# Pooled attention with a routed MLP on one core: the second batch's stores on GpSimd, and another order of all engines' work

## The chip, the cores and the metric

The kernel runs on 1 core of one Trainium2 chip. The metric is device time in microseconds (us): 264.95 us, the median of 3 runs (262.59 to 265.17).

The core has five engines that work beside each other and meet through semaphores. PE (TensorE) multiplies matrices, and its weight loads are listed apart as PEld. DVE (VectorE) and ACT (ScalarE) do elementwise work. POOL (GpSimd) does small elementwise work and issues gathers, scatters and accumulating loads. SP (SyncE) issues plain DMAs. Each engine takes its own instructions strictly in the order of the program: an instruction that waits holds everything that stands behind it on that engine. DMA transfers themselves run on 16 DMA engines that all issuers share.

## What is computed

The input is q, k and v of 8 batches, 8 heads, 576 tokens and a head size of 64, all float32. Keys and values are averaged over groups of 8 tokens, so that 72 pooled ones are left. Each token attends to them. The heads are joined to rows of 512, a gate scores each row, and the 128 best rows of each batch go through a two-layer MLP (512 to 1024 to 512), scaled by a sigmoid of the score and added back.

```
k_p, v_p = mean of k, v over groups of 8 tokens          # 576 -> 72
attn     = softmax(q @ k_p.T / 8) @ v_p                   # per batch and head
x        = attn, heads joined                             # (8, 576, 512)
scores   = x @ w_gate;  top = 128 best tokens per batch
out      = x;  out[top] = x[top] + sigmoid(scores[top]) * (relu(x[top] @ w1) @ w2)
```

## The kernel before

The batches are numbered 0 to 7 here, so the "second batch" is batch 1. Each batch passes two halves.

The **front** of a batch b: its k, q and v are loaded by SP (the last part of v comes in two pieces, of which POOL issues the second, with an add, L346). DVE pools k (L364, L365) and transposes it (L370, L377, L380), transposes q in two halves (L385), and pools v (L423 to L435). PE makes the scores in four quarters (L399), ACT takes their exponentials (L408). A small product centres the gate column (L441). PE then forms the attention output in five chunks (L463; the fifth is a half chunk), ACT and DVE normalise each chunk (L479 to L487) into a result tile `xs`, and each chunk is stored to the output in HBM (L262: four stores of 256 KB and two of 64 KB per batch). From the gate scores (L508 to L515) PE spreads a row over all partitions (L535, two pieces: one of three transposes and one of two), ACT counts ranks (L547), DVE makes a one-hot matrix (L551), PE picks the tokens with it (L560), POOL turns them into row indices (L569) and gathers the 128 chosen rows from HBM (L570). The gather waits until all six stores of its batch have landed.

The **dense half**: PE transposes the gathered rows (L589), multiplies by w1 in eight steps ("up", L597), ACT applies relu (L602), PE multiplies by w2 in eight steps ("down", L606), DVE adds (L611), and POOL scatters the rows back (L615). The weights w1 and w2 are loaded in two halves each. w1's second half is used first.

All these steps are recorded first, as 754 numbered operations with their data dependences (`Plan`), and then emitted in the order that the table `ORDER` gives, so one table sets the order on every engine and on every queue. The table `BANKS` says which bank of PSUM each step takes. The planner knows no times: it places what the table says. 24 small products with zeros (`heat` L278, `fill` L284), which compute nothing, are placed by the table as well, among PE's first work.

Which engine issues a batch's stores is set in `attend`:

```
STORE = ("POOL", "ACT")
...
by = STORE[b] if b < len(STORE) else "SP"
```

So batch 0's stores are issued by POOL, batch 1's by ACT, and those of all others by SP. DMAs that are issued by SP and ACT take turns on one set of eight semaphores (named DMAHW0 to DMAHW7 in the built program), those by POOL on another set of eight (DMASW0 to DMASW7). A DMA whose turn falls on a semaphore is issued only after the DMA that had it before has landed, and its issuer waits for that.

After the scatter of the last batches a range test decides whether a general path has to run; with these inputs it does not.

Of the kernel before, what the change touches and what calls it, by code (L numbers as in the profile page):

```python
# [15 lines left out]
@with_exitstack  # L16
def kernel(
    ctx: ExitStack,
    tc: tile.TileContext,
    q: bass.AP,  # L20
    k: bass.AP,
    v: bass.AP,
    moe_w_gate: bass.AP,
    moe_w1: bass.AP,
    moe_w2: bass.AP,
    moe_capacity,
    out: bass.AP,
):

    nc = tc.nc
    args = (q, k, v, moe_w_gate, moe_w1, moe_w2, moe_capacity, out)
    flag = ctx.enter_context(tc.tile_pool(name="flag", bufs=1)).tile([1, 1], I32, name="flag")
    with ExitStack() as direct:
        direct_path(direct, tc, *args, flag)
    again = nc.values_load(flag[0:1, 0:1], min_val=0, max_val=1)  # L40
    with tc.If(again > 0):
        with ExitStack() as general:
            general_path(general, tc, *args)
# [55 lines left out]


ORDER = [int(x) for x in """
# [27 lines left out]
""".split()]  # L129


BANKS = [int(x) for x in """
# [3 lines left out]
""".split()]  # L136


def direct_path(ctx, tc, q, k, v, moe_w_gate, moe_w1, moe_w2, moe_capacity, out, flag):
# [14 lines left out]
    ROWS = [128] * 4 + [64]  # L154
    HALF = ((0, 16), (16, TG))
    FILL = 16
    STORE = ("POOL", "ACT")
    POOLED = ("DVE",)
    VCUT = ((0, 4), (4, H))
    KCUT = ((0, 12), (12, 24), (24, TG))  # L160
# [287 lines left out]
    def attend(b, c):  # L448
# [46 lines left out]
        rows = out[b].rearrange("(g t) d -> g t d", g=G)  # L495
        by = STORE[b] if b < len(STORE) else "SP"
        if c < 4:
# [544 lines left out]
```

## Time and profile before

| what | before |
|---|---|
| median of 3 runs | 264.95 us (262.59 to 265.17) |
| the profiled execution | 264.21 us, its span 262.3 us |
| PE busy | 234.5 us, 89% of the span |
| DVE, ACT, POOL busy | 133.1, 104.7, 41.2 us |
| moved by DMA | 46.92 MB, 179 GB/s over the span |
| mean granted TensorE clock | 0.962 of full |

The span runs from the first instruction to the last, and 1.9 us lie around it in that execution. In the views a line such as L399 is a line of the kernel, a name such as `xs<-pA,rz` says what an instruction writes and reads, and `x32` that 32 records are taken together (one matrix product with float32 operands leaves two records). "SPq" or "ACTq" is an engine's sequencer, here issuing a DMA. In brackets stands the engine's idle time before the instruction, and who ended it. A granted clock of 1 is 2.4 GHz, 0.5 is 1.2 GHz.

### The profile page before, as it was taken

How to read it: one execution, taken by the hardware profiler on the slowest of the kernel's cores; microseconds unless marked ns; L12 is line 12 of the kernel's file. 1: busy time of each engine (PE TensorE's matmuls, PEld its weight loads, DVE VectorE, ACT ScalarE, POOL GpSimd, SP SyncE). 2: the span in 40 equal slices, each digit the busy share in tenths (PEclk: the TensorE clock that was granted, in tenths of full speed). 3: DMA queues.
4: the chain of work that ended last, by engine and by line, in shares of the span. 5: the costliest groups of instructions: out<-in, count | busy, mean ns of one | idle time of the engine just before them, and what ended most of it. 6: DMA issues, size and time to landing. Idle time of an engine off the chain costs nothing.

```text
span 262.3 us, 7033 instructions
## 1 busy us (share of the span) xinstructions
PE 234.5 (89%) x2994; PEld 179.2 (68%) x2994; DVE 133.1 (51%) x295; ACT 104.7 (40%) x262; POOL 41.2 (16%) x95
## 2 busy tenths in 40 slices
PE   7869969875982999999999998999999999999960
PEld 3348757764982866985689656967796695897420
DVE  4779599967512378569992294753402421100020
ACT  2033426834532466261368316437544453122000
POOL 3001313041001040003110126101101033300020
PEclk9997999999797799999999999999999999999995
DMA  7999999999999069909889974301001751200011
GB/s 216 261 340 285 244 301 347 238 366 340 378 233 339 4 123 329 220 6 317 272 273 281 245 265 100 122 2 42 4 0 42 227 176 40 80 4 1 4 44 42
DMA packets 22454, 46.92 MB, mean 179 GB/s; under 512 B 1904, under 2 KB 12016, under 8 KB 21520
## 3 DMA queue, kind: packets, MB, share of 16 engines
q1 hardware_dynamic: 18864, 38.80, 50.4%
q0 software_dynamic: 2816, 6.42, 9.3%
q10 hardware_dynamic: 736, 1.18, 1.4%
q8 instruction: 25, 0.41, 0.7%
q14 instruction: 13, 0.11, 0.1%
HBM read 34.87 MB, written 11.53 MB: 177 GB/s over the span
## 4 chain that ended last, share of the span: by engine, by line
PE 34%; issue 8%; DMA 4%; POOL 2%; DVE 1%; SPq 1%; POOLq 0%; DVEq 0%
PE pJ L597 13%; PE pJ L606 12%; PE pA L463 3%; PE pS L399 2%; DMA out_dram<-y,ix 2%; DMA vr<-in_v_dram 2%; PE pJ L535 1%; POOL vr L346 1%; PE pJ L589 1%; POOL out_dram L615 1%; SPq L262 1%; DVE y L611 1%; PE pJ L463 0%; POOL xr L570 0%; PE pJ L560 0%
## 5 line engine op out<-in xcount | busy, mean ns | idle before, releaser
L597 PE MATMUL pJ<-xg,w 128*128 128x128 f32 x512 | 63.6, 281 | 0.0
L597 PEld LDWEIGHTS pJ<-xg,w 128*128 128x128 f32 x512 | 60.4, 195 | 3.2 <-issue 1.9
L606 PE MATMUL pJ<-w,ht 128*128 128x512 f32 x128 | 60.1, 604 | 0.0
L408 ACT ACTIVATE et<-pS 128x1024 f32<-128x1024 f32 (+1 forms) x40 | 37.3, 937 | 39.5 <-PE pS L399 39.0
L399 PE MATMUL pS<-qt,kt 32*128 32x128 f32 (+1 forms) x1024 | 42.9, 304 | 3.8 <-issue 2.0
L399 PEld LDWEIGHTS pS<-qt,kt 32*128 32x128 f32 x1024 | 35.6, 192 | 10.0 <-issue 4.4
L463 PEld LDWEIGHTS pA<-vp,et 128*64 128x64 f32 x960 | 32.5, 144 | 6.4 <-issue 2.3
L606 PEld LDWEIGHTS pJ<-w,ht 128*128 128x128 f32 x128 | 22.5, 190 | 20.9 <-issue 20.1
L463 PE MATMUL pA<-vp,et 128*64 128x66 f32 x960 | 36.6, 232 | 0.2 <-issue 0.2
L547 ACT ACTIVATE cmp<-sr,sc 128x576 bf16<-128x576 f32 (+1 forms) x40 | 31.0, 776 | 3.8 <-issue 3.1
L487 DVE TENSOR_TENSOR xs<-pA,rz 128x512 f32<-128x512 f32 x30 | 20.7, 692 | 4.5 <-DVE rz L485 2.0
L385 DVE STREAM_TRANSPOSE qt<-qr 128x1024 f32<-128x1024 f32 (+1 forms) x16 | 21.9, 1368 | 1.0 <-DMA qr<-in_q_dram 1.0
L611 DVE SCALAR_TENSOR_TENSOR y<-pJ,gv,xr 128x512 f32<-128x512 f32 x8 | 6.0, 749 | 29.5 <-PE pJ L606 26.0
L485 DVE RECIPROCAL rz<-za 128x8 f32<-128x8 f32 (+1 forms) x40 | 7.7, 192 | 26.0 <-ACT za L479 25.8
L602 ACT ACTIVATE ht<-pJ 128x512 f32<-128x512 f32 x16 | 9.6, 598 | 26.1 <-PE pJ L597 26.1
L479 ACT ACTIVATE za<-pA,eps 128x8 f32<-128x8 f32 x30 | 8.0, 266 | 22.9 <-PE pA L463 22.6
L615 POOL DMA_INDIRECT out_dram<-y,ix x8 | 8.4, 1047 | 48.4 <-DVE gv L579 24.9
L569 POOL TENSOR_SCALAR ix<-tg 128x1 int32<-128x1 f32 x8 | 1.9, 237 | 83.4 <-DVE tg L565 82.3
L535 PE MATMUL pJ<-ident,sc 128*128 128x128 f32 (+1 forms) x40 | 8.3, 289 | 5.5 <-DVE sc L515 5.4
L540 ACT COPY sr<-pJ 128x192 f32<-128x192 f32 (+1 forms) x16 | 6.4, 398 | 15.5 <-PE pJ L535 15.5
L364 DVE TENSOR_TENSOR kr<-kr 128x1152 f32<-128x1152 f32 (+1 forms) x10 | 11.1, 1111 | 2.5 <-DMA kr<-in_k_dram 2.5
L346 POOL DMA_DIRECT2D vr<-in_v_dram x8 | 7.7, 1008 | 28.8 <-DMA vr<-in_v_dram 28.8
(84 smaller groups left out, 198.5 us busy)
## 6 DMA issues: line engine op xcount, KB each, us to landing
kr<-in_k_dram SPq DMA_DIRECT2D x7, 1152.0 KB, 11.4
vr<-in_v_dram SPq DMA_DIRECT2D x8, 896.0 KB, 15.1
out_dram<-xs SPq DMA_DIRECT2D x24, 256.0 KB, 5.2
qr<-in_q_dram SPq DMA_DIRECT2D x8, 640.0 KB, 11.8
qr<-in_q_dram SPq DMA_DIRECT2D x8, 512.0 KB, 11.3
w<-in_moe_w_dram SPq DMA_DIRECT2D x4, 1024.0 KB, 16.4
kr<-in_k_dram SPq DMA_DIRECT2D x3, 384.0 KB, 4.0
vr<-in_v_dram SPq DMA_DIRECT2D x8, 128.0 KB, 8.3
```

The costliest lines, as they stand in the source:

```text
L346: nc.gpsimd.dma_start(out=x[TWO:128], in_=rows_v(b, TWO + 1, 128 - TWO, 2), accum_op=OP.add)
L364: e.tensor_tensor(out=x[:, a:z, 0:2], in0=x[:, a:z, 0:2], in1=x[:, a:z, 2:4], op=OP.add)
L385: nc.vector.transpose(out=QT[b % 2][h].rearrange("p j s (t g) -> p t (j s) g", g=G), in_=QR[b % 2][h].rearrange("p t (j s g) -> p t (j s) ...
L399: nc.tensor.matmul(pS[:, i, 256 * s : 256 * s + n], KT[b % 2][p, j, s, :], QT[b % 2][h][p, j, s, x : x + n], start=(j == 0), stop=(j == 1))
L408: nc.scalar.activation(ET[c][b % NB[c]].rearrange("p n (g t) -> p n g t", g=G), pS.rearrange("p i (s x) -> p (i s) x", s=2)[:, :, y : y + ...
L463: nc.tensor.matmul(o[d][64 * w : 64 * w + 64, E * y : E * y + E], et[:, 2 * m + s, 64 * u : 64 * u + 64], VP[i][:, 2 * m + s, :], start=Tr ...
L487: nc.vector.tensor_tensor(out=XS[i][c].rearrange("p (m s d) -> p s m d", s=2, d=D)[:, k], in0=o[:, :, :, 0:D], in1=rz.rearrange("p (s m on ...
L535: nc.tensor.transpose(row[:, OFF[c] - OFF[a] : OFF[c] - OFF[a] + n], SC[i][0:n, c : c + 1].to_broadcast([n, 128]), ident[0:n, 0:n])
L547: nc.scalar.activation(cmp[0:n], SR[0:n], AF.Sign, bias=SC[i][0:n, c : c + 1], scale=-1.0, accum_out=RK[0:n, b, c])
L597: nc.tensor.matmul(acc[:, cap * f : cap * f + cap], w1[g][:, d, 128 * f : 128 * f + 128], XG[i][:, d, :], start=(d == 0), stop=(d == DB - 1))
L606: nc.tensor.matmul(job(ds)[0:cap, :], HT[i][f // 4][:, f % 4, :], w2[f // 4][:, f % 4, :], start=(f == 0), stop=(f == FB - 1))
L615: j = nc.gpsimd.indirect_dma_start(out=out_rows, out_offset=bass.IndirectOffsetOnAxis(ap=IX[x][:, :1], axis=0), in_=Y[i], in_offset=None)
```

## The change

The stores of batch 1 are issued by POOL instead of ACT, and the two tables are replaced as a whole. No operation is added or taken away, and none changes its size. The diff, with a line or two of each table:

```diff
 ORDER = [int(x) for x in """
-33 27 28 2 30 0 35 36 37 42 38 43 31 39 40 44 41 1 108 47 45 46 32 34 111 62 5 3 15 8 4 63 58 59 110 109 9 14
+2 28 33 27 4 19 14 9 35 36 37 16 18 12 17 30 7 31 42 43 44 0 32 34 38 39 6 21 25 24 40 41 45 46 47 1 108 48
...
 BANKS = [int(x) for x in """
-3 3 3 3 3 3 3 3 1 2 1 1 1 2 1 2 1 1 1 1 2 2 2 2 3 3 3 3 1 0 1 0 0 1 2 1 2 3 3 3 3 2 0 1 0 0 1 2 1 1 1 2 1 1 3
+3 3 3 3 3 3 3 3 2 1 1 1 2 1 1 1 1 1 1 1 1 1 1 1 3 3 3 3 1 0 0 0 1 1 1 2 2 3 3 3 3 1 0 0 0 0 1 2 1 2 2 1 2 2 3
...
-    STORE = ("POOL", "ACT")
+    STORE = ("POOL", "POOL")
```

On POOL the six stores of batch 1 now stand behind that batch's own small work (L520 to L524) and ahead of the accumulating load of batch 4 and of batch 1's gather.

The first place is ACT around batch 1's last stores. The rows name in brackets the semaphores that an instruction waits for. `xs_98` to `xs_102` are batch 1's five result chunks, `ss_103` the gate scores of batch 2, `et` the exponentials of batch 3, `cmp` the rank counts of batch 1. Before:

```order
L602 ACTIVATE ht_132<-pJ_163 128x512 [waits PE_49]
L262 DMA out_dram<-xs_100 16x8x512 [waits DMAHW0_49]
L408 ACTIVATE et_83<-pS 128x1024 [waits PE_49]
L262 DMA out_dram<-xs_98 16x8x512 [waits DMAHW4_49]
L262 DMA out_dram<-xs_99 16x8x512 [waits DMAHW6_49]
L547 ACTIVATE cmp,rk<-sr,sc_108 128x576 [waits Activation_49]
L262 DMA out_dram<-xs_102 16x4x256 [waits DMAHW0_49]
L511 COPY ss_103<-ss_103 64x4 [waits DVE_49]
L262 DMA out_dram<-xs_101 16x8x512 [waits DMAHW1_49]
L408 ACTIVATE et_85<-pS 128x1024 [waits PE_49]
```

With the change:

```order
L547 ACTIVATE cmp,rk<-sr,sc_108 128x576 [waits Activation_49]
L547 ACTIVATE cmp,rk<-sr,sc_108 64x576 [waits Activation_49]
L602 ACTIVATE ht_132<-pJ_164 128x512 [waits PE_49]
L408 ACTIVATE et_87<-pS 128x1024 [waits PE_49]
L479 ACTIVATE za<-pA,eps 128x8 [waits DVE_49,PE_49]
L480 COPY ss_103<-pA 128x8
L511 COPY ss_103<-ss_103 64x4
L479 ACTIVATE za<-pA,eps 128x8 [waits DVE_49,PE_49]
L480 COPY ss_103<-pA 128x8
```

What moved: the stores are gone from ACT, and the copy of `ss_103` (L511), which DVE needs for batch 2's row scores, no longer stands behind a DMA that waits for a DMAHW semaphore.

The second place is PE between batch 0's pick (L560, `oh`) and the transposes of its gathered rows (L589, `xr_125`). `vp_91` and `vp_90` are the pooled values of batch 1 and batch 2, `qt_78` and `qt_79` the two halves of batch 2's q, `pJ_163` and `pJ_164` two PSUM banks. Before:

```order
L560 MATMUL pJ_164<-aux_110,oh 128x9
L284 MATMUL pJ_163<-zero 128x256
L463 MATMUL pJ_163<-vp_91,et_85 64x66 x8
L463 MATMUL pJ_164<-vp_91,et_85 64x66 x8
L463 MATMUL pA<-vp_90,et_84 64x66 x16
L399 MATMUL pS<-qt_79,kt_76 128x192 x16
L463 MATMUL pA<-vp_90,et_86 64x66 x16
L535 MATMUL pJ_163<-ident,sc_108 128x128
L535 MATMUL pJ_163<-ident,sc_108 128x64
L589 MATMUL pJ_163<-ident,xr_125 128x128 x4
```

With the change, where one quarter of scores and one chunk of attention (`qt_78`, `et_88`) stand between the pick and the first row here:

```order
L284 MATMUL pJ_163<-zero 128x256
L399 MATMUL pS<-qt_79,kt_76 128x128 x16
L441 MATMUL pJ_163<-vp_90,share 128x8
L463 MATMUL pA<-vp_91,et_87 64x66 x16
L399 MATMUL pS<-qt_79,kt_76 128x192 x16
L535 MATMUL pJ_163<-ident,sc_108 128x128
L535 MATMUL pJ_163<-ident,sc_108 128x64
L535 MATMUL pJ_164<-ident,sc_108 128x128 x3
L463 MATMUL pA<-vp_90,et_82 64x66 x16
L463 MATMUL pJ_163<-vp_90,et_89 64x66 x8
L589 MATMUL pJ_164<-ident,xr_125 128x128 x4
```

What moved: the pick now stands ahead of six steps of batches 1 and 2 that it stood behind, and behind one chunk (`et_85`) that it stood ahead of. Between it and the transposes stand three quarters of scores and three full chunks of attention, where there were one quarter and three chunks.

The third place is SP where the weights are loaded: `w_138` and `w_137` are the second and the first half of w1, `w_139` and `w_140` those of w2, `kr`, `qr`, `vr` parts of k, q and v of batches 3 and 4. Before:

```order
L262 DMA w_138<-in_moe_w_dram 128x4x512
L262 DMA qr_70<-in_q_dram 128x1024
L262 DMA w_137<-in_moe_w_dram 128x4x512
L262 DMA qr_71<-in_q_dram 128x1280
L262 DMA w_139<-in_moe_w_dram 128x4x512
L262 DMA kr<-in_k_dram 128x2304
L262 DMA w_140<-in_moe_w_dram 128x4x512
L262 DMA qr_68<-in_q_dram 128x1024
L262 DMA vr_72<-in_v_dram 16x8x256
L262 DMA vr_72<-in_v_dram 112x8x256
```

With the change:

```order
L262 DMA w_138<-in_moe_w_dram 128x4x512
L262 DMA qr_71<-in_q_dram 128x1280
L262 DMA vr_73<-in_v_dram 112x8x256
L262 DMA w_137<-in_moe_w_dram 128x4x512
L262 DMA kr<-in_k_dram 128x2304
L262 DMA vr_72<-in_v_dram 16x8x256
L262 DMA w_139<-in_moe_w_dram 128x4x512
L262 DMA qr_68<-in_q_dram 128x1024
L262 DMA vr_72<-in_v_dram 112x8x256
L262 DMA w_140<-in_moe_w_dram 128x4x512
```

What moved: each weight half now stands behind more of the loads of batches 3 and 4, the last half of w2 behind batch 4's whole v.

## Rows read from the trace of the kernel before

**Rows 1.** 10 us stretches: engines busy (instructions); granted clock, DMA share, GB/s.
```profile
20.00:30.00 10.00, 9.76 (x198) 8.24 (x200) 8.53 (x16) 3.67 (x11) 0.96 (x2) 0.83 1.17 233
30.00:40.00 10.00, 7.96 (x158) 6.48 (x158) 7.70 (x14) 3.87 (x9) 3.78 (x7) 1.00 1.07 319
60.00:70.00 10.00, 6.98 (x86) 6.32 (x83) 6.05 (x12) 5.43 (x18) 1.01 (x5) 0.83 1.05 358
80.00:90.00 10.00, 6.65 (x88) 6.09 (x92) 3.44 (x6) 4.32 (x11) 1.01 (x5) 0.66 0.50 177
90.00:100.00 10.00, 10.00 (x127) 6.25 (x120) 6.97 (x14) 6.38 (x19) 3.23 (x4) 1.00 0.62 142
```

**Rows 2.** PE's timeline at 34 us: start, length, instruction [idle before, releaser].
```profile
34.96 0.94 PE L399 MATMUL pS<-qt,kt 32*128 32x128 f32 x21 [1.98 <-issue]
```

**Rows 3.** Timeline of all engines, 71 to 86 us; ACTq issues DMAs.
```profile
71.72 0.56 ACTq L262 DMA_DIRECT2D out_dram<-xs  x1
...
82.29 0.55 ACTq L262 DMA_DIRECT2D out_dram<-xs  x1
82.87 0.19 ACT L511 COPY ss<-ss 64x4 f32<-64x4 f32 x1 [5.00 <-DMA out_dram<-xs]
...
83.10 0.20 DVE L515 TENSOR_REDUCE sc<-ss 128x5 f32<-128x40 f32 x1 [6.88 <-ACT ss L511]
...
83.35 0.90 PE L535 MATMUL pJ<-ident,sc 128*128 128x128 f32 x3 [5.39 <-DVE sc L515]
...
84.05 1.91 PE L597 MATMUL pJ<-xg,w 128*128 128x128 f32 x8
...
85.89 2.09 PE L399 MATMUL pS<-qt,kt 32*128 32x128 f32 x32
```

**Rows 4.** DMA issues in four short stretches: KB each, us from issue to landing.
```profile
out_dram<-xs ACTq DMA_DIRECT2D x1, 256.0 KB, 10.5
...
xr<-out_dram,ix POOLq DMA_INDIRECT x1, 8.9
...
w<-in_moe_w_dram SPq DMA_DIRECT2D x1, 1024.0 KB, 17.5
...
vr<-in_v_dram SPq DMA_DIRECT2D x1, 896.0 KB, 18.7
```

**Rows 5.** SP's timeline: the issues of the last two transfers of Rows 4.
```profile
49.66 1.16 SPq L262 DMA_DIRECT2D w<-in_moe_w_dram  x1
...
61.19 1.36 SPq L262 DMA_DIRECT2D vr<-in_v_dram  x2
```

**Rows 6.** PE's timeline: the first centring, batch 0's pick and its gathered rows.
```profile
19.53 0.36 PE L441 MATMUL pJ<-vp,share 128*128 128x8 f32 x2 [2.52 <-DVE vp L435]
...
52.99 0.37 PE L560 MATMUL pJ<-aux,oh 128*128 128x9 bf16 x5
...
63.81 0.63 PE L589 MATMUL pJ<-ident,xr 128*128 128x128 f32 x4 [2.88 <-DMA xr<-out_dram,ix]
```

**Rows 7.** Timeline, 161 to 163 us.
```profile
161.51 0.75 DVE L611 SCALAR_TENSOR_TENSOR y<-pJ,gv,xr 128x512 f32<-128x512 f32 x1 [3.44 <-DMA out_dram<-y,ix]
...
162.32 0.39 PE L441 MATMUL pJ<-vp,share 128*128 128x8 f32 x2 [1.23 <-DVE gv L578]
```

**Rows 8.** Chain of waits, 182 to 206 us: PE's steps at full clock.
```profile
182.26 1.10 PE pS L399 x32
...
187.32 1.51 PE pS L399 x32
...
189.91 1.09 PE pJ L597 x8
...
200.19 1.08 PE pA L463 x32
...
205.65 1.05 PE pJ L606 x2
```

**Rows 9.** Line 262: POOL's stores, shortest/median/longest ns, first and last start.
```profile
L262 POOL DMA_DIRECT2D out_dram<-xs x6: 525/544/567, 29.9 to 39.6; - x6
```

56 rows, old and new, of tables (BANKS, ORDER) are left out of this document.

## The prediction

> **What bounds the kernel now.** I read the stretches first, then PE's timeline for its waits, then that of all engines around the longest of them. In the stretches [rows 1] PE is busy for all of 90 to 100 us, while the DMA engines are at 0.62: from there on the loads are ahead, and PE's own work sets the pace until the end. Before that the reader is to see two things: PE is busy for only 6.65 us of 80 to 90 and 6.98 of 60 to 70, and in the same stretches its granted clock is 0.66 and 0.83 of full. So the price of a wait is the wait itself and the half-speed work behind it.
>
> The longest wait is 5.39 us, at 83.35 [rows 3]. PE's spread of batch 2's row scores waits for DVE's sum, that for ACT's copy of the gate scores (L511), and that stood on ACT behind a store of batch 1. This store was issued at 82.29. The store issued at 71.72 had the same DMAHW semaphore and took 10.5 us to land [rows 3, 4], until 82.2. So ACT did nothing for 5.00 us because a DMA semaphore came round. The two next longest waits are 2.88 us for batch 0's gathered rows and 2.52 us for the first centring [rows 6].
>
> The sum is made against the profiled execution, 264.21 us with a span of 262.3. It is 0.74 below the median of the runs. I leave that inside the range.
>
> **The change part by part.** All of PE's, DVE's and ACT's operations stay as many and as large. After 90 us PE has one wait left, of 1.2 us [rows 7], so what is saved before it moves the end by as much.
>
> *Batch 1's stores off ACT.* The wait of 5.39 goes. With it goes the half-speed work: the spread took 0.90 for three transposes, the up step 1.91 and the scores 2.09 [rows 3], where an up step takes 1.09 and a quarter of scores 1.10 at full clock [rows 8]. That is 0.82 and 0.99, and half of 0.90 on the spread: 2.3. What is late next? The sum's other inputs are products that DVE makes itself; in the new order the first spread piece of batch 2 stands behind batch 1's pick and two more up steps, so I cost the remainder at 0. Together **-7.7**. Bounds: 0 if another wait takes the place, -7.7 at most.
>
> *The same six stores on POOL.* POOL issues a store in 0.525 to 0.567 us [rows 9], six in 3.3. POOL is busy for 1.01 us of 60 to 70 and of 80 to 90 [rows 1], so this lies beside other work. What is queued behind them on POOL are the accumulating load of batch 4, batch 1's gather and batch 2's small work. The gather must land before batch 1's transposes on PE. Between batch 1's pick and those the new order has two up steps, three chunks, two quarters and eight down steps among others, 2 x 1.09 + 3 x 1.08 + 2 x 1.10 + 8 x 1.05 = 16.0 us by [rows 8]. From batch 0's pick to its transposes it took 63.81 - 52.99 = 10.8 us [rows 6], with the DMA engines full. So 5.2 us of cover are left: **0**.
>
> The six stores that POOL issued before [rows 9] fell mostly into 30 to 40 us, where DVE was busy for 7.70 of 10 us [rows 1], and they lie within 8% of each other. The Trainium skill, "SBUF — State Buffer", section "SBUF: two separate sides", speaks against this change: DMAs issued from GpSimd need it to write their descriptors, it is locked out while VectorE runs certain operations, and such a DMA of about 620 ns then takes about 3100. By that page six stores would hold POOL for an estimated 18.6 us instead of 3.3, and the sum would be up to 10.1 us higher, by what exceeds the cover. The trace does not agree so far: no store of POOL shows it.
>
> *Batch 0's gathered rows.* The chain from pick to transposes took 10.8 us, most of it the gather's 8.9 us to land [rows 4, 6]. In the new order three quarters of scores (1.10, 1.10, 1.51), three chunks (1.08 each) [rows 8] and six small steps lie between. The small ones I estimate at 2.1 us, from the pick's 0.37 [rows 6] and the 0.90 at half clock for three transposes [rows 3]. That is 9.05, so 1.8 of wait remain and 1.1 go. With them goes the slow clock behind the wait: 0.83 over 10 us is 1.7 us [rows 1], of which I take 1.5, since PE was not busy throughout. I take it whole, because PE also waited 1.98 us at 34.96 [rows 2], and 30 to 40 us kept the full clock [rows 1], while 2.52, 2.88 and 5.39 were each followed by a slow one. **-2.6**. Bounds: 0, if the gather lands that much later with more stores on the way, and -4.4.
>
> *The first centring.* The new order puts the third quarter of scores of batch 0 ahead of it, 1.10 us of work that stood behind [rows 8]. The wait of 2.52 falls to 1.4, and by the same reasoning the slow clock of 20 to 30 us (0.83) [rows 1] goes: 1.5. **-2.6**. Bounds: 0, if the q transpose that this quarter needs comes late on DVE and PE only waits one step earlier, and -4.0.
>
> *The wait on a scatter.* At 162.32 PE waits 1.23 us behind DVE, which had waited 3.44 for batch 0's scatter to land before it could write its buffer again [rows 7]. On POOL that scatter stood behind batch 3's gather, batch 1's scatter and an accumulating load. Now it directly follows the gather, and between batch 3's pick and the end of batch 2's down steps PE has eight score and attention steps, where it had two. **-1.2**. Bounds: 0 to -1.2.
>
> *The weights, a new wait.* Every half of w1 and w2 stands later on SP. Before, w2's first half was issued at 49.66 and took 17.5 us, to 67.2; batch 4's v was issued by 62.5 at the latest and took 18.7, to at most 81.2 [rows 4, 5]. In the new order w1's first half has the same loads but one weight half ahead of it as the former had, w2's last half as much as the latter. Batch 1's stores, 1.15 MB, now go out before them: at 358 GB/s [rows 1] 3.2 us more. So they land by 70.4 and 84.4. When does PE ask? Batch 0's pick comes ahead of two quarters and three chunks and behind one: 2 x 1.10 + 2 x 1.08 = 4.4 us earlier, at 48.6, the transposes 10.8 later, at 59.4. The fifth up step follows three quarters, three chunks and four up steps, some 11 us: 70. The fifth down step follows four more up steps, three quarters, four chunks and four down steps, some 17: 87. A small wait is likely at the first, none at the second. The bounds are 0 and 3.5; I take **+1.0**, nearer to the lower end, since PE comes to each half at about its landing or later.
>
> The opening's zero products, the pause inside a step [rows 2] and the last four steps with the scatters behind them stay: 0 each, the pause of 2.0 both ways as a bound.
>
> The sum: 264.2 - 7.7 - 2.6 - 2.6 - 1.2 + 1.0 = **251.1**.
>
> **The rivals.** *The loads become the bound.* At 20 to 40 and 60 to 70 us the DMA engines are over 1.0 [rows 1], and the new order asks for batch 3's front and the weights in the same stretch. Two waits of 2.5 us at weights or scores, each with 1.5 of slow clock, give 251.1 + 8 = 259. For it: the DMA share. Against: at 80 to 90 it is 0.50 already. Chance 0.18, times 255 to 262.
>
> *POOL's issues go slow.* If POOL could write an issue only while DVE idles, six stores of 3.3 us would take 8.3 us where DVE is busy for 6.05 of 10 us, and 22 where it is busy for 8.53 [rows 1]: 5 to 19 us more, less the cover of 5.2, so 251 to 265, some 258 in the middle. Against: [rows 9], which were taken under a busy DVE. Chance 0.04. The rule of the Trainium skill, "SBUF — State Buffer", section "SBUF: two separate sides", is of this kind.
>
> *The change doesn't save what it says*: the loads, not ACT, set when 83 us is reached, and everything only waits elsewhere: 264. For it: batch 4's v lands close to that time, at 81. Against: the one long wait of that stretch was for ACT [rows 3]. Chance 0.06.
>
> *Slower: weights behind buffers on SP.* The last half of w2 now stands behind batch 4's q and v, which wait until batch 2's are no longer read. If DVE frees those late, SP holds the weights too, and PE stands at the fifth down step of batch 0 with nothing else allowed past. It decides from the point at which that half lands 16.5 us after PE's arrival, at 103.5 instead of 84.4: then 251.1 + 16.5 = 267.6. For it: such transfers took 17.5 and 18.7 us to land [rows 4], so that a late issue is paid in full. Against: DVE has to pool batch 2's v before any chunk of batch 2, which PE does before the first up step. With the half-speed work behind such a wait, 270. Chance 0.06.
>
> **The numbers.** My forecast has 0.66, and its own range is 246 to 255: below, the gathered rows' last 1.8, the +1.0 and the pause of 2.0 fall away; above, one of the two 2.6 terms stays and so does 1.3 more of weights. The range for 8 in 10 takes in both 2.6 terms lost and weights at 3.5, 251.1 + 2.6 + 2.6 + 2.5 = 258.8, which also covers over half of the first rival: 246 to 259. A measurement of this kernel can tell about 1% from no change, 2.6 us: 262.3 to 267.6. Faster: 0.66, 0.17 of the first rival and 0.03 of the second, 0.86. Same: the third, with the rest of the first two, 0.08. Slower: 0.06.
>
> **What would show it.** In the profile of the changed kernel ACT issues no DMA, and no copy of gate scores waits for one; the spread of batch 2 waits under 1 us. The stores on POOL take about 0.55 us each. The wait before batch 0's transposes is under 2 us, that before the first centring under 1.5, and 60 to 70 us and 80 to 90 us have a granted clock of 1.0. PE is busy throughout some 10 us sooner than at 90. Wrong it is if PE waits over 2 us for a weight half, if batch 1's gather is issued long after its pick, or if PE, though it is through batch 3's front early, waits for batch 5's loads.

## The result: 250.83 us, and where the 13.6 us came from

The changed kernel takes **250.83 us** (median of 4 runs, 249.48 to 255.33) against 264.42 beside it, a ratio of 0.948, with a 95% interval of 0.940 to 0.955. Measured again (e9) it took 251.54 (6 runs), 0.952 (0.948 to 0.957). The forecast was 251.1, with a range of 246 to 259. Some executions of most kernels here are over 1.5% above the fastest of the same kernel; the ratios leave them out, and the profiles of e1, e8 and e12 below are of such ones.

The profiled execution took 249.48 us, with a span of 247.7 and a mean granted clock of 0.991. The stretches come first, with the columns of [rows 1]:

```profile
20.00:30.00 10.00, 9.21 (x202) 7.02 (x198) 9.16 (x17) 4.01 (x13) 1.73 (x3) 1.00 1.08 286
30.00:40.00 10.00, 7.57 (x150) 5.97 (x146) 7.98 (x14) 4.95 (x11) 4.79 (x12) 1.00 1.06 300
...
60.00:70.00 10.00, 10.00 (x204) 9.21 (x197) 7.76 (x16) 7.67 (x21) 0.00 (x0) 1.00 1.03 398
...
80.00:90.00 10.00, 10.00 (x145) 6.42 (x144) 6.05 (x12) 3.17 (x7) 0.95 (x1) 1.00 0.86 272
90.00:100.00 10.00, 10.00 (x113) 9.20 (x113) 4.09 (x9) 5.70 (x15) 0.00 (x0) 1.00 1.04 282
```

The granted clock was 0.83, 0.83 and 0.66 at 20, 60 and 80 us [rows 1] and is 1.00 now. PE is full from 60 us on, while it was busy for 6.98 and 6.65 us of the stretches at 60 and 80. PE's timeline, at the places of [rows 3, 6]:

```profile
16.98 1.17 PE L399 MATMUL pS<-qt,kt 32*128 32x128 f32 x32 [1.63 <-DVE qt L385]
...
18.99 0.36 PE L441 MATMUL pJ<-vp,share 128*128 128x8 f32 x2 [0.21 <-DVE vp L435]
...
45.65 0.37 PE L560 MATMUL pJ<-aux,oh 128*128 128x9 bf16 x5 [0.45 <-DVE oh L551]
...
58.44 0.63 PE L589 MATMUL pJ<-ident,xr 128*128 128x128 f32 x4 [1.41 <-DMA xr<-out_dram,ix]
...
69.52 2.05 PE L597 MATMUL pJ<-xg,w 128*128 128x128 f32 x16
...
76.41 0.47 PE L535 MATMUL pJ<-ident,sc 128*128 128x128 f32 x2
...
86.61 0.54 PE L535 MATMUL pJ<-ident,sc 128*128 128x128 f32 x3
86.99 2.74 PE L606 MATMUL pJ<-w,ht 128*128 128x512 f32 x6
```

Both pieces of batch 2's spread (L535) start without a wait, where 5.39 us stood. The wait for batch 0's gathered rows is 1.41 us (2.88), that before the first centring 0.21 (2.52), but 1.63 now stands before the quarter that was put ahead of it. Neither half of the weights is waited for, at 69.52 (L597) and 86.99 (L606). The wait of 1.23 at 162 us [rows 7] is gone.

POOL, DVE and SP in the stretch of batch 1's stores:

```profile
56.15 3.17 POOL L262 DMA_DIRECT2D out_dram<-xs  x6
```
```profile
56.21 1.24 DVE L385 STREAM_TRANSPOSE qt<-qr 128x1024 f32<-128x1024 f32 x1
```
```profile
61.99 7.03 SPq L262 DMA_DIRECT2D w<-in_moe_w_dram  x1
```

Six stores in 3.17 us are 0.53 each, as in [rows 9], with DVE at work beside them. SP's issue of w2's last half, against that, took 7.03 us.

The span fell by 14.6 us. PE's busy time fell by 7.1, from 234.5 to 227.4, with the same products. In the three slow stretches of before PE was busy for 12.2 us at a granted clock of 0.50, which is 6.1 us lost, and the zero products went from 20.3 to 18.7 us. PE's idle time fell from 27.8 to 20.3: the four waits of [rows 3, 6, 7] went from 12.0 to 3.25, and the rest, of which the end behind PE's last product is 0.8, grew by 1.3.

### The profile page after: what moved, and what is told of

It is laid out like the page before. It is cut to its first block, busy times and chain, and to the rows that moved or that the text cites. A ratio compares the mean times of both kernels' runs of the same rounds, so it can differ in the third digit from the quotient of the medians.

```text
span 247.7 us, 7047 instructions
## 1 busy us (share of the span) xinstructions
PE 227.4 (92%) x2994; PEld 173.9 (70%) x2994; DVE 132.6 (54%) x294; ACT 104.2 (42%) x260; POOL 45.3 (18%) x101
## 4 chain that ended last, share of the span: by engine, by line
PE 71%; DMA 16%; issue 5%; DVE 3%; POOL 2%; SPq 1%; POOLq 0%; DVEq 0%
PE pJ L597 24%; PE pJ L606 22%; PE pA L463 10%; PE pS L399 10%; DMA vr<-in_v_dram 9%; DMA xr<-out_dram,ix 4%; DMA kr<-in_k_dram 2%; PE pJ L535 2%; PE pJ L589 2%; DMA out_dram<-y,ix 1%; PE pJ L463 1%; PE pJ L560 1%; POOL out_dram L262 1%; SPq L262 1%; DVE xs L487 1%
## 5 line engine op out<-in xcount | busy, mean ns | idle before, releaser
L597 PE MATMUL pJ<-xg,w 128*128 128x128 f32 x512 | 62.0, 278 | 0.0
L597 PEld LDWEIGHTS pJ<-xg,w 128*128 128x128 f32 x512 | 59.2, 192 | 3.1 <-issue 2.2
L606 PE MATMUL pJ<-w,ht 128*128 128x512 f32 x128 | 59.8, 602 | 0.0
L399 PE MATMUL pS<-qt,kt 32*128 32x128 f32 (+1 forms) x1024 | 41.3, 296 | 3.5 <-DVE qt L385 2.4
L399 PEld LDWEIGHTS pS<-qt,kt 32*128 32x128 f32 x1024 | 34.3, 185 | 10.6 <-issue 4.0
L463 PE MATMUL pA<-vp,et 128*64 128x66 f32 x992 | 36.0, 225 | 1.6 <-DVE xs L487 0.9
L606 PEld LDWEIGHTS pJ<-w,ht 128*128 128x128 f32 x128 | 22.5, 190 | 20.4 <-issue 19.8
L463 PEld LDWEIGHTS pA<-vp,et 128*64 128x64 f32 x992 | 31.7, 137 | 7.1 <-issue 3.1
L487 DVE TENSOR_TENSOR xs<-pA,rz 128x512 f32<-128x512 f32 x31 | 21.5, 692 | 5.0 <-DVE rz L485 2.0
L479 ACT ACTIVATE za<-pA,eps 128x8 f32<-128x8 f32 x31 | 8.3, 267 | 23.9 <-PE pA L463 23.2
L551 DVE TENSOR_TENSOR oh<-slots,rk 128x640 bf16<-128x640 f32 x8 | 6.6, 823 | 13.7 <-ACT cmp L547 13.7
L423 DVE TENSOR_TENSOR vr<-vr 128x1024 f32<-128x1024 f32 (+1 forms) x9 | 9.8, 1099 | 4.4 <-DMA vr<-in_v_dram 4.4
## 6 DMA issues: line engine op xcount, KB each, us to landing
qr<-in_q_dram SPq DMA_DIRECT2D x8, 640.0 KB, 10.8
w<-in_moe_w_dram SPq DMA_DIRECT2D x4, 1024.0 KB, 24.6
```

Source lines behind the costliest of these rows:

```text
L399: nc.tensor.matmul(pS[:, i, 256 * s : 256 * s + n], KT[b % 2][p, j, s, :], QT[b % 2][h][p, j, s, x : x + n], start=(j == 0), stop=(j == 1))
L423: e.tensor_tensor(out=x[:, a:z, 0:2], in0=x[:, a:z, 0:2], in1=x[:, a:z, 2:4], op=OP.add)
L463: nc.tensor.matmul(o[d][64 * w : 64 * w + 64, E * y : E * y + E], et[:, 2 * m + s, 64 * u : 64 * u + 64], VP[i][:, 2 * m + s, :], start=Tr ...
L479: nc.scalar.activation(ZA[:, b, z0 : z0 + nz].rearrange("p (s m) -> p s m", s=2)[:, k], o[:, :, :, D], AF.Identity, bias=eps)
L487: nc.vector.tensor_tensor(out=XS[i][c].rearrange("p (m s d) -> p s m d", s=2, d=D)[:, k], in0=o[:, :, :, 0:D], in1=rz.rearrange("p (s m on ...
L597: nc.tensor.matmul(acc[:, cap * f : cap * f + cap], w1[g][:, d, 128 * f : 128 * f + 128], XG[i][:, d, :], start=(d == 0), stop=(d == DB - 1))
```

## The experiments

Ratios are to the kernel before, measured beside each; a ratio turned into a time is that share of 264.4 us, so that 0.971 is 256.7. e1 to e4 ran on one chip, e5 to e8 on a second, e9 to e12 on a third, so that between these groups a difference of the times and one of the ratios need not agree. The ratios of e5 to e8 rest on three executions of the kernel before (258.76, 262.53 and 262.61 us), which lie lower than in the other groups, so that these ratios may read up to 1% high.

### e1: the stores alone

```diff
-    STORE = ("POOL", "ACT")
+    STORE = ("POOL", "POOL")      # kernel before, its own ORDER and BANKS
```

> The old order with only batch 1's stores given to POOL. Theory (the terms add): the wait of 5.39 us before batch 2's spread goes with its half-speed work, 7.7 us, the waits before batch 0's transposes (2.88) and before the first centring (2.52) stay, and so do the half-clock stretches behind them: 264.4 - 7.7 = 256.7 us, 255 to 259. Rival 1 (the order is needed for it, since on POOL the six stores now stand ahead of batch 1's one-hot pieces and gather): 261 us or more, with a wait over 2 us before batch 1's transposes. Rival 2 (the issuer is nearly all of the change: fewer DMAs share the semaphores of SP's loads, so that SP's loads come sooner too): 250 to 253 us, with PE's waits before 83 us shorter than in the kernel before although the order is the same.

Measured: 0.971 (0.963 to 0.979), **256.7 us**. The theory holds, with the size it gave. PE's waits in the profile:

```profile
19.90 0.36 PE L441 MATMUL pJ<-vp,share 128*128 128x8 f32 x2 [1.98 <-DVE vp L435]
...
65.85 1.09 PE L589 MATMUL pJ<-ident,xr 128*128 128x128 f32 x4 [3.47 <-DMA xr<-out_dram,ix]
...
79.81 0.54 PE L535 MATMUL pJ<-ident,sc 128*128 128x128 f32 x3
```

The spread of batch 2 (79.81) doesn't wait; the other two waits stay.

### e2: the order alone

```diff
-    STORE = ("POOL", "POOL")
+    STORE = ("POOL", "ACT")       # changed kernel, its own ORDER and BANKS
```

> The new order with batch 1's stores left on ACT, where they stand in one block of six behind the copy of batch 2's gate scores. Theory (the terms add): the waits before batch 0's transposes, before the first centring and at 162 us are as in the changed kernel, 1.4, 0.2 and 0 us; the copy for batch 2's spread stands ahead of the stores, so the spread doesn't wait, but what stands behind them on ACT (batch 3's last exponentials, batch 0's second relu) waits up to 5 us: 250.8 + 5 to 7.7 = 256 to 258.5 us. Rival 1 (the order alone does it): within 1% of the changed kernel, 249 to 253. Rival 2 (ACT's stores share the eight semaphores with SP's loads and each waits for an older DMA to land, so the block of six holds ACT for over 8 us): 260 us or more.

Measured: 1.000 (0.994 to 1.006), **no gain at all**: rival 2. Up to 60 us this execution is much like the changed kernel, with its transposes at 59.13 after a wait of 1.23, though its granted clock is 0.93 and 0.89 from 10 to 30 us. Then ACT's timeline shows two of the six stores and what stood behind them:

```profile
82.62 0.55 ACTq L262 DMA_DIRECT2D out_dram<-xs  x1
...
85.01 0.55 ACTq L262 DMA_DIRECT2D out_dram<-xs  x1
...
87.22 0.27 ACT L479 ACTIVATE za<-pA,eps 128x8 f32<-128x8 f32 x1 [16.35 <-DMA out_dram<-xs]
```

SP's issue of w2's last half, that load's time to landing, and PE behind it:

```profile
58.33 8.45 SPq L262 DMA_DIRECT2D w<-in_moe_w_dram  x1
```
```profile
w<-in_moe_w_dram SPq DMA_DIRECT2D x1, 1024.0 KB, 24.3
```
```profile
88.56 2.03 PE L463 MATMUL pA<-vp,et 128*64 128x66 f32 x32 [9.25 <-DVE xs L487]
```

The load lands at 58.33 + 24.3 = 82.6, and the store at 82.62 goes out then, though it has nothing to do with that load and stands on another engine. In the trace both use the same semaphore. So ACT was held for 16.35 us and PE for 9.25.

### e3: two of ACT's stores later, in the old order

```diff
 L547 ACTIVATE cmp,rk<-sr,sc_108 128x576
-L262 DMA out_dram<-xs_102 16x4x256
 L511 COPY ss_103<-ss_103 64x4
-L262 DMA out_dram<-xs_101 16x8x512
 ...
 L408 ACTIVATE et_89<-pS 128x512
+L262 DMA out_dram<-xs_102 16x4x256
+L262 DMA out_dram<-xs_101 16x8x512
```

> The old order with batch 1's last two stores moved on ACT from in front of the copy of batch 2's gate scores to behind batch 3's last exponential; the other four stay. Theory (one store's wait for one semaphore is the 5.39 us): the spread of batch 2 waits under 1 us and the time falls by 5.4 to 7.7, to 257 to 259 us. Rival (SP's loads and the stores share the semaphores, so the wait goes to another store or to a load and PE waits for it some steps later): 261 to 265, with a new wait of over 3 us between 75 and 95 us.

Measured: 0.990 (0.984 to 0.996), 261.8 us: 2.6 us (1.0 to 4.2 by the interval) of the 5.4 to 7.7. ACT, DVE and PE of this profile:

```profile
76.60 0.78 ACT L547 ACTIVATE cmp<-sr,sc 128x576 bf16<-128x576 f32 x1 [2.60 <-DMA out_dram<-xs]
```
```profile
82.20 0.69 DVE L487 TENSOR_TENSOR xs<-pA,rz 128x512 f32<-128x512 f32 x1 [2.79 <-DMA out_dram<-xs]
```
```profile
82.95 1.15 PE L463 MATMUL pA<-vp,et 128*64 128x66 f32 x32 [2.30 <-DVE xs L487]
...
97.50 0.63 PE L589 MATMUL pJ<-ident,xr 128*128 128x128 f32 x4 [1.34 <-DMA xr<-out_dram,ix]
```

The rival was nearer, in smaller waits than its 3 us. An earlier store now holds ACT; DVE waits to write a result tile of batch 3 until a store of batch 1 has left that buffer; and batch 1's gather, which needs all six stores landed, is late. So three things wait for a late store: what stands behind it on ACT, DVE's next write to its buffer, and the gather of its batch. Moving two of the six only changes which of them comes last.

### e4: the stores on SP, in the new order

```diff
-    STORE = ("POOL", "POOL")
+    STORE = ("POOL", "SP")        # changed kernel
```

> The new order with batch 1's stores on SP, where they stand between w2's last half and batch 4's second q. Theory (what mattered is that ACT issues no DMA): ACT is free, the stores only delay batch 4's second q and batch 5's v by their issues, 6 x 0.6 = 3.6 us, which come back as at most one wait of 2 to 3 us: 251 to 254 us. Rival (the semaphores that SP's loads share with the stores are what matters, POOL having its own): each store on SP waits until an older DMA has landed and the loads behind wait too, two waits of over 2.5 us on PE at 75 to 105 us with slow clock behind: 256 to 260.

Measured: 0.971 (0.961 to 0.981), 256.8 us, in the rival's range; of its waits there is one of 4.48 us, not two of 2.5. The first of the six stores needed 15.6 us to land (issued at 67.64), and DVE and PE waited for it:

```profile
out_dram<-xs SPq DMA_DIRECT2D x1, 256.0 KB, 15.6
```
```profile
83.36 0.69 DVE L487 TENSOR_TENSOR xs<-pA,rz 128x512 f32<-128x512 f32 x1 [8.26 <-DMA out_dram<-xs]
```
```profile
84.10 2.03 PE L463 MATMUL pA<-vp,et 128*64 128x66 f32 x32 [4.48 <-DVE xs L487]
```

In the changed kernel POOL's four large stores took 9.1 us in the median, and all six had landed by 69 us:

```profile
out_dram<-xs POOLq DMA_DIRECT2D x4, 256.0 KB, 9.1
```

So it was not enough that ACT issues none. POOL's stores leave early (from 56.15 instead of 67.64), beside SP's loads instead of behind them.

### e5: the first centring back ahead of the quarter

```diff
+L441 MATMUL pJ_163<-vp_90,share 128x8
 L399 MATMUL pS<-qt_79,kt_76 128x128 x16
 L284 MATMUL pJ_163<-zero 128x256
-L441 MATMUL pJ_163<-vp_90,share 128x8
```

> The changed kernel with batch 0's centring put back ahead of the third quarter of its scores on PE; nothing else moves. Theory of the prediction's step (the 2.52 us wait and the half-clock stretch behind it cost 2.6 us in full): the wait is back at 2.0 to 2.6 us, the granted clock of 20 to 30 us falls below 0.9, and the time rises by 1.9 to 3.6 us, to 252.7 to 254.4. Rival (until 58 us PE waits for DVE and for loads anyway, so that what is lost at 19 us is taken back from the later waits of 0.73, 1.57 and 1.41 us): within 1 us of the changed kernel, 250 to 251.8, with the transposes of batch 0's gathered rows at the same 58 to 59 us.

Measured: 254.74 us, against 251.54 of the changed kernel in e9; ratios 0.974 (0.963 to 0.985) and 0.952. It costs 3.2 us by the times, more by the ratios. The theory holds in its direction, and the lost time isn't taken back, but the wait came to 3.66 us where 2.0 to 2.6 were expected, and the time is 0.3 above the theory's range:

```profile
19.67 0.57 PE L441 MATMUL pJ<-vp,share 128*128 128x8 f32 x2 [3.66 <-DVE vp L435]
...
63.35 0.63 PE L589 MATMUL pJ<-ident,xr 128*128 128x128 f32 x4 [1.47 <-DMA xr<-out_dram,ix]
```
```profile
20.00:30.00 10.00, 9.93 (x150) 7.68 (x151) 6.29 (x12) 3.38 (x9) 1.68 (x2) 0.70 1.08 251
```

The clock behind the wait of 3.66 is 0.70.

### e6: batch 0's transposes earlier

```diff
+L589 MATMUL pJ_164<-ident,xr_125 128x128 x4
 L535 MATMUL pJ_163<-ident,sc_108 128x128
 ...
 L463 MATMUL pA<-vp_90,et_82 64x66 x16
 L463 MATMUL pJ_163<-vp_90,et_89 64x66 x8
-L589 MATMUL pJ_164<-ident,xr_125 128x128 x4
```

> The changed kernel with batch 0's transposes of gathered rows put on PE ahead of batch 1's second spread and of two chunks of batch 2 (1.0 + 1.15 + 0.7 us of work that then stands behind the wait). Theory (the gather's landing sets this wait, and what stands behind it is lost in full): the wait grows from 1.4 to over 4 us, the time by 2.8 us, and by up to 1.7 more if half-clock work follows: 253.6 to 255.3. Rival (loads and DVE after 58 us have slack that takes it up, or the chain behind is not PE's): 250 to 252.

Measured: 0.969 (0.949 to 0.989); its three lowest times are 252.87 to 253.53 us, and the five lowest of the changed kernel in e9 are 250.25 to 252.23, some 2 us less. The direction is the theory's, the size below its 2.8. The edit also puts the first piece of batch 1's spread into the other's PSUM bank, and PE waits 0.41 us for that at 58.48. The wait grew to 3.38 us, not to 4, since the rows landed sooner here:

```profile
57.11 0.66 PE L589 MATMUL pJ<-ident,xr 128*128 128x128 f32 x4 [3.38 <-DMA xr<-out_dram,ix]
```

### e7 and e11: the zero products between the steps

The new order has four of the 512-column zero products between the steps of batches 0 and 1, at 23.2 and 39.5 us. e7 puts them back into the opening, e11 leaves them out.

```diff
+L278 MATMUL pS<-zero 128x512   x4   (e7: behind the first one; e11: not at all)
 ...
 L463 MATMUL pJ_164<-vp_90,et_88 64x66 x8
-L278 MATMUL pS<-zero 128x512
 ...
-L278 MATMUL pS<-zero 128x512   x3
```

> The changed kernel with the four zero products of 512 columns that stand between batch 0's and batch 1's steps (at 23.2 and at 39.5 to 42.3 us) put back into the opening, where the old order had them. Theory (they only fill time in which PE would wait for ACT's and DVE's ranks, and keep the clock up): PE waits 2 to 3 us before batch 0's pick in their place, the pick itself comes no sooner than 45 us, and a stretch at half clock behind costs 0 to 1.7 us: 250.5 to 252.6. Rival 1 (they cost their 3.8 us): 247 to 248. Rival 2 (the opening is on the path, and four more products there make it later): 253 or more.

> The changed kernel without the four zero products of 512 columns (1.1 us at 23.2 and 2.8 us at 39.5 to 42.3); they feed nothing. Theory (they stand where PE would wait for ranks and for DVE anyway and keep the clock up): a wait of 2 to 3 us before batch 0's pick, half-clock work behind it, 0 to 1.7 us slower than the changed kernel: 250.5 to 252.5. Rival (they only cost time): 247 to 249.

Measured: e7 252.72 us, 0.968 (0.958 to 0.978); e11 **250.01 us, 0.943** (0.938 to 0.949), against 0.952 (0.948 to 0.957) of the changed kernel beside it. e7 lies 0.1 us above the theory's range, and its profile shows what the theory asks for, a wait of 2.57 before the pick and a clock of 0.91 and 0.92 from 40 to 60 us:

```profile
47.90 0.37 PE L560 MATMUL pJ<-aux,oh 128*128 128x9 bf16 x5 [2.57 <-DVE oh L551]
```

In e11 the clock stayed at 1.00 in every stretch up to 100 us although PE waited:

```profile
36.26 0.39 PE L441 MATMUL pJ<-vp,share 128*128 128x8 f32 x2 [2.29 <-DVE vp L435]
...
46.86 0.37 PE L560 MATMUL pJ<-aux,oh 128*128 128x9 bf16 x5 [0.87 <-DVE oh L551]
...
59.27 0.63 PE L589 MATMUL pJ<-ident,xr 128*128 128x128 f32 x4 [1.04 <-DMA xr<-out_dram,ix]
```

From batch 0's spread to its pick PE takes 7.1 us with the three products at 39.5 us (38.52 to 45.65 in the first profile, 40.48 to 47.62 in e9) and 7.1 without them (39.71 to 46.86 in e11), where it waits in their place, three times, 3.3 us in all. So these three fill a wait, as the theory says, and cost nothing there; that the clock needs them e11 doesn't bear out. By its median and its ratio e11 is the fastest version of all, 1.5 us below the changed kernel by the times and 2.4 by the ratios. That it beats it is likely, not certain, since the intervals touch, and where the gain would come from the profiles don't show.

### e8: two more waits filled

```diff
-L441 MATMUL pJ_163<-vp_91,share 128x8
 L284 MATMUL pJ_164<-zero 128x256
 L399 MATMUL pS<-qt_81,kt_77 128x192 x16
+L441 MATMUL pJ_163<-vp_91,share 128x8
 ...
+L399 MATMUL pS<-qt_80,kt_77 128x128 x16
 L589 MATMUL pJ_164<-ident,xr_125 128x128 x4
-L399 MATMUL pS<-qt_80,kt_77 128x128 x16
```

> The changed kernel with two of its remaining waits filled: the last quarter of batch 1's scores ahead of its centring (wait 1.57 us at 35.1), and the first quarter of batch 3's scores ahead of batch 0's transposes (wait 1.41 us at 58.4). Theory (every wait of PE before 60 us that is filled with work moves the end by as much): 248.0 to 249.6. Rival (only the second lies on the path, since the chain through ranks, pick and gather sets when PE gets there): 249.4 to 250. Rival 2 (the waits come up again at the next step): 250.3 to 251.3.

Measured: 251.16 us, 0.960 (0.948 to 0.971). No gain can be told: rival 2 by its size. In the profiled execution, of 256.78 us, neither of the two places has a wait of more than 0.51 us, but PE waits elsewhere, for w2's last half among others:

```profile
94.33 2.84 PE L606 MATMUL pJ<-w,ht 128*128 128x512 f32 x6 [1.43 <-DMA w<-in_moe_w_dram]
```

### e9: the changed kernel again

> The changed kernel itself once more, as the measure for the runs beside it. All theories: 249.5 to 251.5 us; no wait of PE over 2 us after the first 10 us, and a granted clock of 1.0 in each stretch up to 100 us, except where a run happens to wait longer.

Measured: 251.54 us. Three of PE's waits were longer than in the first profile, with the clock at 1.00 throughout the first 100 us, so the expectation of none over 2 us was wrong:

```profile
13.38 1.17 PE L399 MATMUL pS<-qt,kt 32*128 32x128 f32 x32 [2.34 <-DVE qt L385]
...
37.03 0.39 PE L441 MATMUL pJ<-vp,share 128*128 128x8 f32 x2 [2.40 <-DVE vp L435]
...
60.81 0.63 PE L589 MATMUL pJ<-ident,xr 128*128 128x128 f32 x4 [1.82 <-DMA xr<-out_dram,ix]
```

The same kernel reaches batch 0's transposes at 58.44 and at 60.81: single waits before 60 us vary by 1 to 2 us. From there to the last long row of PE (L606, at 224.43 and 226.30) it takes 166.0 and 165.5 us, so that what differs between the two ends is made before 60 us.

### e10: the stores and one part of the order

```diff
-    STORE = ("POOL", "ACT")
+    STORE = ("POOL", "POOL")      # kernel before, and on PE:
+L399 MATMUL pS<-qt_79,kt_76 128x128 x16
 L441 MATMUL pJ_163<-vp_90,share 128x8
-L399 MATMUL pS<-qt_79,kt_76 128x128 x16
```

> The old order with batch 1's stores on POOL (256.5 us by its ratio) and one more thing of the new order: the third quarter of batch 0's scores ahead of the first centring on PE. Theory (this term of the prediction, 2.6 us: 1.1 of work into the wait, and the half-clock stretch behind it gone): 253 to 255 us, the wait before the centring under 1.5 us, a granted clock over 0.95 in 20 to 30 us. Rival (it pays only together with the rest of the new order, as the order did with ACT's stores): 256 to 257.5, with the time lost again before batch 0's transposes, whose wait is 3 us or more there.

Measured: 0.983 (0.978 to 0.988), 259.9 us: not faster than e1, rather slower. Neither was right. The wait before the centring is 0.25, with 1.15 before the quarter, and 20 to 30 us has the full clock, as the theory wanted. But PE waits and pauses later, so that nothing is won, though before the transposes it waits only 1.69, not the rival's 3:

```profile
26.39 1.15 PE L463 MATMUL pA<-vp,et 128*64 128x66 f32 x32 [1.72 <-DVE xs L487]
...
34.54 0.94 PE L399 MATMUL pS<-qt,kt 32*128 32x128 f32 x21 [2.24 <-issue]
...
57.15 0.49 PE L463 MATMUL pJ<-vp,et 128*64 128x66 f32 x5 [1.38 <-issue]
...
64.74 0.63 PE L589 MATMUL pJ<-ident,xr 128*128 128x128 f32 x4 [1.69 <-DMA xr<-out_dram,ix]
```

The pauses at 34.54 and 57.15 have their like in the kernel before (1.98 at 34.96, 1.40 at 56.35), so of these it is the 1.72 that is new. What took the whole 2.6 us back is not shown.

### e12: the weights' margin

```diff
+L262 DMA qr_69<-in_q_dram 128x1280
 L262 DMA w_140<-in_moe_w_dram 128x4x512
-L262 DMA qr_69<-in_q_dram 128x1280
```

> The changed kernel with w2's last half behind batch 4's second q on SP, one load of 640 KB later. Theory (the half landed only some 0.5 us before PE asked for it, at 87.0): it now lands 1.5 to 3 us later, PE waits 1 to 2.5 us before batch 0's fifth down step, and with half-clock work behind the longer of these the time rises by 1 to 4 us: 251.8 to 254.8. Rival (the half is there early, as the prediction's 84.4 has it): no wait, 250 to 251.5.

Measured: 0.953 (0.947 to 0.959), as the changed kernel. But this ratio rests on three of the six times (249.95 to 252.76). The other three are 254.61 to 254.91, in the theory's range or just above it, where the changed kernel had 2 of 10 so high. In one of them, the profiled one, PE waited for that half:

```profile
89.77 5.49 PE L606 MATMUL pJ<-w,ht 128*128 128x512 f32 x6 [2.87 <-DMA w<-in_moe_w_dram]
```

So the experiment doesn't decide between theory and rival: whether it is this wait that made three of the times so long stays open.

## Why the prediction was right, step by step

| step | predicted | measured, profiled execution |
|---|---|---|
| wait before batch 2's spread | -5.4 | -5.4 |
| half-speed work, all stretches | -5.3 (2.3 + 1.5 + 1.5) | -7.1 of PE's busy time, 6.1 of it in the three stretches |
| wait for batch 0's gathered rows | -1.1 | -1.5 (e9: -1.1) |
| first centring | -1.1 | -0.7 (0.21 + 1.63 against 2.52) |
| wait on a scatter | -1.2 | -1.2 |
| weights | +1.0 | 0 |
| the rest | 0 | +1.3 |
| sum | -13.1 | -14.6 of the span; -13.6 by the medians |

*Batch 1's stores off ACT, -7.7.* Shown by e1, by the same amount. The forecast blamed one store and one semaphore. e2 and e3 show more: a store on ACT waits for whatever had its semaphore before, a load of SP that takes 24 us included, and neither of the two other places tried on ACT was good. The rival that the loads and not ACT set when 83 us is reached falls with e1.

*The six stores on POOL, 0.* Right: 0.53 us each, and batch 1's gather went out at 75.92, 1.7 us after its pick at 74.23. The slow issues that the Trainium skill, "SBUF — State Buffer", section "SBUF: two separate sides", warns of did not come; the page ties them to certain operations of VectorE, and in that stretch DVE ran a transpose, a reciprocal and a product out of PSUM, as the records show. How a copy between SBUF tiles would act no run here shows.

*The order's terms, -5.4 together.* Given the stores on POOL the order brings 256.7 - 250.8 = 5.9 us (4 to 8 by e1's interval), as forecast. But the step failed in one respect: the terms were added as if each stood alone. With the stores on ACT the order brings nothing: it packs them into one block there, and ACT is held for 16.35 us (e2). The centring's term costs 3.2 us or more when it is undone (e5) and brings nothing when it is done alone (e10). Its detail came out in part at the bound that the prediction named, a wait one step earlier, on DVE's transpose of q. The term of the scatter was not tried alone.

*Batch 0's gathered rows.* That the wait came out at 1.41, near the 1.8 worked out, is luck. From the pick to the transposes it took 58.44 - 45.65 = 12.8 us, where the 10.8 of before was taken over: the gather landed in 9.2 us (8.9 before), but was issued 3.5 us after the pick (1.8 before). PE's steps between, with two waits of 0.5, took 11.4 us where 9.05 was added up. Both misses are about 2 us, and they cancel.

*The half-speed work.* Under-sized by 0.8 by the three stretches, by 1.8 by PE's whole busy time. All three slow stretches went, each as its wait went or shrank, and one came back with a longer wait: 0.70 behind 3.66 us (e5). But e9 and e11 kept 1.00 with waits of 2.29 to 2.40, and e1 fell to 0.83 behind 1.98, so that the length of a wait alone doesn't tell whether it costs the clock.

*The zero products* were costed at 0 as part of the opening. The new order moves four of them out of it: by the times e7 puts that move at about 1 us of gain. In the profiles three of them stand in a wait and cost nothing (e11).

*The weights, +1.0.* Not seen, and in part by luck. PE came to the halves at 69.52 and 86.99, where 70 and 87 were expected, but the halves did not land when worked out:

```profile
41.75 1.09 SPq L262 DMA_DIRECT2D w<-in_moe_w_dram  x1
```
```profile
w<-in_moe_w_dram SPq DMA_DIRECT2D x1, 1024.0 KB, 24.6
```
```profile
86.49 0.54 SPq L262 DMA_DIRECT2D out_dram<-xs  x1
```

w1's first half was there at 41.75 + 24.6 = 66.4, 4 us sooner than the 70.4 worked out. w2's last half was there only at 86.47, 2 us later than the 84.4: the store at 86.49 is SP's next issue on that load's semaphore, and SP waited 3.7 us for it. A margin of 2.6 us was worked out, and 0.5 was left (1.4 in e9). In the profiles of e8 and e12 PE waits for this half, 1.43 and 2.87 us, so the prediction's first rival, that the loads become the bound, was near.

*The signs.* PE was full some 30 us sooner, not 10: once its wait for batch 0's rows ends at 58.44, nothing stops it, since the next wait was the 5.39.

## What to carry to other kernels

A DMA queue is chosen with its semaphores: a store that takes turns with long loads can wait for one of them to land, and holds its engine's compute meanwhile, wherever it stands. Price two coupled changes as a pair: the issuer alone brought 7.7 us, the order alone 0, both 13.6. And a wait is dear by the slow clock that may follow it, which here was not much less than the waits themselves: 6.1 us at half clock went, and 8.8 of waits.

## What the runs showed of the hardware

- A store on ACT went out within 0.02 us of the landing of a load that SP had issued 24.3 us earlier (e2).
- With the DMA engines full, POOL's stores landed in 9.1 us, a store that SP issued some 10 us later behind its loads in 15.6 (e4), and w2's half in 24.3 (e2).
- An issue on SP itself took 7.03 us (changed kernel) and 8.45 (e2), where SP's issues in the changed kernel have medians of 0.4 to 0.8.
- PE stops inside a step, with no releaser that the trace names, at the same place in all four profiles of the old order: 1.98 us up to 34.96 in the kernel before [rows 2], 1.98 in e1, 1.43 in e3 and 2.24 in e10. Around its start, 32.98 in the kernel before, the trace has a 16 KB packet of the queue that it lists as "instruction", from 32.40 to 33.51; another ends at 54.95, where PE's next such pause (1.40) begins. So PE may have waited for its own program. That was not tried.
